# Moving TensorE's streamed operand as single elements taken in turn from its two halves

## The chip, the core and the metric

The kernel runs on one core of a Trainium2 chip. The metric is the device time of one execution in microseconds (us). The core has five engines that work side by side: TensorE (PE, matrix products), VectorE (DVE), ScalarE (ACT), GpSimd (POOL) and SyncE (SP, which issues most transfers). A matrix product on TensorE has two operands from SBUF: a block of 128x128 that is loaded into the array first (LDWEIGHTS, "PEld" in the profile), and a second one, up to 512 columns wide, that is moved through the array column by column (MATMUL, "PE"). The result lands in PSUM, from where VectorE or ScalarE read it.

## The reference

```python
def reference(q, k, v, w_in, w_out, s, b, w_gate, w1, w2):
    # masked attention: 4 batches, 8 heads, 576 positions, 64 dims
    scores = np.where(masks, q @ k.T / 8, -1e9)       # first 4 heads local, last 4 strided
    x = softmax(scores) @ v                           # -> [2304, 512]
    h = x @ w_in                                      # 512 -> 2048
    x2 = (s * np.maximum(h, 0) ** 2 + b) @ w_out      # 2048 -> 512
    logits = x2 @ w_gate                              # 8 experts, 288 tokens each, greedy by logit
    for e in range(8):
        out[mine(e)] = np.maximum(x2[mine(e)] @ w1[e], 0) @ w2[e]   # 512 -> 1024 -> 512
    return out
```

## The kernel before

Matrix products need more precision than one pass gives, so each float32 operand is split into a rounded high part and a low part (type float32r, 4 bytes per element), and three products (high x high, high x low, low x high) are summed in PSUM. All large products work in this way.

The order of the work is written out by hand, with generators that are advanced step by step (`Pipe`), so each engine's instructions stand in the order in which the code emits them. There are these stages:

- Attention (`attn_unit`, lines 222 to 312), in 32 units, beside the preparation of `w_in` and `w_out` (`prep`, lines 360 to 425). It uses many small matmuls.
- The first layer, `h_step` (lines 457 to 479): for each of 6 groups of 384 tokens and each of 16 blocks of 128 features, 12 matmuls at line 464 move a block of x (128x384). ScalarE reads PSUM with Relu (line 469), squares (line 470), and the result goes to a DRAM buffer `ud`.
- The second layer, `late_step` and `x2_late` (lines 638 to 684): `ud` comes back, is split (lines 653, 656), and line 683 issues the matmuls that `x2_list` (line 509) lists; they move a half-row block of `w_out` (128x512). Forty-eight of them are held for the end of this stage and are issued at line 895. `x2_row` (line 515) reads PSUM on VectorE (line 519). Beside this runs the choice of tokens for each expert (`route`, lines 729 to 863), whose small matmuls and VectorE steps are placed between those of line 683.
- Eight experts: `layer1` (line 935) issues 12 matmuls for each of 8 feature blocks (line 941, moving 128x288), `relu_split` (line 946) reads PSUM on ScalarE (line 947) and VectorE (line 948), and `expert` (line 950) issues 12 matmuls more for each block (line 966, moving 128x288), whose results are copied out at lines 974 and 976. The last expert (`last_expert`, line 996) has the second layer the other way round: line 1004 moves 128x512 of w2, and the results are copied out in two halves (lines 1009 and 1010).

All of these move their operand in the order in which it lies in SBUF. PSUM buffers are 8 tiles of 128x512, used in turn (`ps`, line 134).

Elsewhere the kernel has operands that are not read or written in the order in which they lie: `prep` reads the high or low word of pairs (lines 372, 378, 381: a step of 8 bytes), `attn_unit` writes the strided heads' results into `xb` with a step of 16 elements (line 310), and some reductions read across columns (lines 420 and 536 from PSUM, 757, 758 and 823 from SBUF).

Of the kernel before, what the change touches and what calls it, by code (L numbers as in the profile page):

```python
# [12 lines left out]
AF = mybir.ActivationFunctionType  # L13
ALU = mybir.AluOpType
# [14 lines left out]

def _f(ap):  # L30
    return ap.bitcast(F32)


class Pipe:
# [28 lines left out]
class Body:  # L63
# [262 lines left out]
    def group_x(self, g, dc):  # L326
        nc = self.nc
        S, G = self.S, self.G
        h = self.xs.tile([128, G], F32R, tag="xh", name=self.nm("xh"))
        l = self.xs.tile([128, G], F32R, tag="xl", name=self.nm("xl"))  # L330
        t = g * G
        while t < (g + 1) * G:
            b = t // S
            e = min((b + 1) * S, (g + 1) * G)
            src = self.xb[b][:, dc, t - b * S:e - b * S]
            o = slice(t - g * G, e - g * G)
            nc.scalar.copy(h[:, o], src)
            nc.vector.tensor_tensor(l[:, o], src, _f(h[:, o]), op=ALU.subtract)
            t = e
        self.xg.setdefault(g, {})[dc] = h, l  # L340
# [10 lines left out]
    def split(self, W, put):  # L351
        nc = self.nc
        h = self.wt([128, 512], F32R, "wh")
        l = self.wt([128, 512], F32R, "wl")
        nc.scalar.copy(h, W)  # L355
        yield
        nc.vector.tensor_tensor(l, W, _f(h), op=ALU.subtract)  # L357
        put((h, l))

    def prep(self, i):  # L360
# [10 lines left out]
        for r, h in zip(rv, half):  # L371
            nc.scalar.activation(_f(K[:, h]), _f(r[:, :, 1]), AF.Abs)
# [84 lines left out]
    def h_step(self, g, fc):  # L457
        nc = self.nc
        wh, wl = self.win[fc]
        ps = self.ps()  # L460
        k = 0
        for w, x in ((wh, 0), (wh, 1), (wl, 0)):
            for dc in range(4):
                nc.tensor.matmul(ps[:, :self.G], w[:, dc * 128:(dc + 1) * 128], self.xg[g][dc][x],  # L464
                                 start=(k == 0), stop=(k == 11))
                k += 1
        yield
        r = self.wt([128, self.G], F32, "r")
        nc.scalar.activation(r, ps[:, :self.G], AF.Relu)  # L469
        nc.scalar.activation(r, r, AF.Square)  # L470
        yield
        nc.sync.dma_start(self.ud[g][fc], r)
        if g in self.DG:
            return
        yield
        self.fold_step(fc, g, r)
        if fc == 15:
            yield
            yield from self.logits(g, self.pf[g])
# [28 lines left out]

    def x2_list(self, fc, acc, u, t=0):
        wh, wl = self.wout[fc]  # L510
        return [dict(out=acc[t + k], lhsT=u[:, j, k * 128:(k + 1) * 128], rhs=w,
                     start=(fc == 0 and i == 0), stop=(fc == 15 and i == 2))
                for k in range(u.shape[2] // 128) for i, (j, w) in enumerate(((0, wh), (0, wl), (1, wh)))]

    def x2_row(self, g, t, acc):
        nc = self.nc
        i = g * 3 + t
        row = self.Es[i % self.NE].rearrange("p c k -> p (c k)")
        nc.vector.scalar_tensor_tensor(row, acc[t], self.sb[:, 0:1], self.acc, op0=ALU.mult, op1=ALU.add)  # L519
        nc.sync.dma_start(self.x2d[i * 128:(i + 1) * 128, :], row)  # L520
        return row

# [412 lines left out]
    def layer1(self, fc, X, w1):  # L935
        ps = self.ps()
        fh, fs = fc // 4, (fc % 4) * 128
        k = 0
        for wi, xi in ((0, 0), (0, 1), (1, 0)):
            for dc in range(4):  # L940
                self.nc.tensor.matmul(ps[:, :288], w1[dc, fh][wi][:, fs:fs + 128], X[:, xi, dc, :],  # L941
                                      start=(k == 0), stop=(k == 11))
                k += 1
        return ps

    def relu_split(self, ps, h, l):
        self.nc.scalar.activation(h, ps[:, :288], AF.Relu)  # L947
        self.nc.vector.scalar_tensor_tensor(l, ps[:, :288], 0.0, _f(h), op0=ALU.max, op1=ALU.subtract)  # L948

    def expert(self, e, X, w1, w2):  # L950
        nc = self.nc
        y = []

        def step(fc):
            ps = self.layer1(fc, X, w1)
            yield
            u = self.p2.tile([128, 2, self.G], F32R, tag="u", name=self.nm("u2"), bufs=self.UB)
            self.relu_split(ps, u[:, 0, :288], u[:, 1, :288])
            yield
            if fc == 0:  # L960
                y.extend(self.ps() for _ in range(4))
            wh, wl = w2[fc]
            for dc in range(4):
                sl = slice(dc * 128, (dc + 1) * 128)
                for i, (w, j) in enumerate(((wh, 0), (wh, 1), (wl, 0))):
                    nc.tensor.matmul(y[dc][:, :288], w[:, sl], u[:, j, :288], start=(fc == 0 and i == 0),  # L966
                                     stop=(fc == 7 and i == 2))
            if fc < 7:
                return
            yT = []  # L970
            for dc in range(4):
                t = self.wt([128, 288], F32, "yT")
                if dc % 2:
                    nc.vector.tensor_copy(t, y[dc][:, :288])
                else:
                    nc.scalar.copy(t, y[dc][:, :288])
                yT.append(t)
            yield
            for c in range(3):
                ps = self.ps()  # L980
                for dc in range(4):
                    nc.tensor.transpose(ps[:96, dc * 128:(dc + 1) * 128], yT[dc][:, c * 96:(c + 1) * 96], self.identf)  # L982
                t = self.wt([96, 512], F32, "yr")
                if c % 2:
                    nc.vector.tensor_copy(t, ps[:96, :])
                else:
                    nc.scalar.copy(t, ps[:96, :])
                nc.gpsimd.indirect_dma_start(
                    out=self.a["out"][:, :],
                    out_offset=bass.IndirectOffsetOnAxis(ap=self.idx[:, 3 * e + c:3 * e + c + 1], axis=0),  # L990
                    in_=t, in_offset=None)
                yield

        return (step(fc) for fc in range(8))

    def last_expert(self, e, X, w1, w2):
        nc = self.nc
        us, y = [], []

        def layer2(fc, c):  # L1000
            if fc == 0:
                y.append(self.ps())
            for i, (j, w) in enumerate(((0, 0), (0, 1), (1, 0))):
                nc.tensor.matmul(y[c][:96, :], us[fc][j][:, c * 96:(c + 1) * 96], w2[fc][w],  # L1004
                                 start=(fc == 0 and i == 0), stop=(fc == 7 and i == 2))

        def put(c):
            t = self.Es[c].rearrange("p c k -> p (c k)")[:96]
            nc.scalar.copy(t[:, :256], y[c][:96, :256])
            nc.vector.tensor_copy(t[:, 256:], y[c][:96, 256:])  # L1010
            nc.gpsimd.indirect_dma_start(
                out=self.a["out"][:, :],
                out_offset=bass.IndirectOffsetOnAxis(ap=self.idx[:, 3 * e + c:3 * e + c + 1], axis=0),
                in_=t, in_offset=None)

        def step(fc):
            ps = self.layer1(fc, X, w1)
            yield
            u = [self.wt([128, 288], F32R, "u3") for _ in range(2)]
            self.relu_split(ps, u[0], u[1])  # L1020
            us.append(u)
            yield
            layer2(fc, 0)
            if fc == 7:
                put(0)
                for c in (1, 2):
                    for f in range(8):
                        layer2(f, c)
                    put(c)

        return (step(fc) for fc in range(8))
# [105 lines left out]
```

## Time and profile before

| | |
|---|---|
| median of 3 runs | 795.71 us (793.93 to 796.56) |
| the profiled execution | 795.12 us, of which span 793.3 us |
| TensorE busy | 771.1 us (97%), 6436 matmuls |
| weight loads busy | 677.9 us (85%) |
| VectorE busy | 493.4 us (62%) |
| ScalarE busy | 371.3 us (47%) |
| GpSimd busy | 52.4 us (7%) |
| mean granted TensorE clock | 0.992 |

The profile is one execution seen by the hardware profiler. The span runs from the first to the last instruction. Lines (L464) are lines of the kernel. Matmuls are pipelined, so a matmul's own duration holds its way through the array; the pace of a stream of them is read from their starts.

### The profile page before, as it was taken

What the parts mean: (1) busy time and instruction counts of PE and PEld (TensorE: products, weight loads), DVE (VectorE), ACT (ScalarE), POOL (GpSimd) and SP (SyncE); (2) the same over time, 40 slices, a digit from 0 to 9 for tenths busy, and PEclk for the clock granted to TensorE, in tenths of its full rate; (3) what the DMA queues carried; (4) which work ended last, traced back from release to release, by engine and by line L of the source; (5) the groups of instructions that cost most, each with busy time, mean ns of one, the idle gap of its engine ahead of it and who ended that gap; (6) DMA issues with size and microseconds to landing.
All of it is one profiled execution on the core that took longest, in us unless ns stands there. A gap on an engine that the chain in (4) does not pass through costs nothing.

```text
span 793.3 us, 16902 instructions
## 1 busy us (share of the span) xinstructions
PE 771.1 (97%) x6436; PEld 677.9 (85%) x6436; DVE 493.4 (62%) x1229; ACT 371.3 (47%) x893; POOL 52.4 (7%) x69
## 2 busy tenths in 40 slices
PE   7979999999999999999989999999999999999996
PEld 5769999999999878887767777778999999999994
DVE  8788997997650233267767778775456465555620
ACT  3787675666664554422222222230355454555520
POOL 1000000000000000000000000001102211321211
PEclk9989999999999999999999999999999999999999
DMA  6967846765774995535233523252857656755411
GB/s 175 266 212 239 265 139 201 239 207 189 250 260 170 318 300 195 165 120 175 91 132 122 177 89 100 81 160 68 239 169 222 208 162 213 214 176 170 130 31 30
DMA packets 88753, 140.19 MB, mean 177 GB/s; under 512 B 10849, under 2 KB 52577, under 8 KB 88673
## 3 DMA queue, kind: packets, MB, share of 16 engines
q1 hardware_dynamic: 85600, 129.68, 51.3%
q0 software_dynamic: 3072, 9.44, 3.7%
q8 instruction: 50, 0.82, 0.4%
q14 instruction: 31, 0.25, 0.1%
HBM read 106.32 MB, written 32.77 MB: 175 GB/s over the span
## 4 chain that ended last, share of the span: by engine, by line
PE 88%; DVE 4%; DMA 4%; ACT 1%; issue 1%; SPq 0%; POOLq 0%; DVEq 0%
PE b L464 25%; PE b L683 19%; PE b L941 13%; PE b L966 11%; PE b L242 3%; DMA r<-ud 3%; PE b L301 2%; PE b L502 2%; PE b L1004 1%; PE b L895 1%; PE b L982 1%; DVE E L519 1%; PE b L318 1%; PE b L397 1%; PE b L280 1%
## 5 line engine op out<-in xcount | busy, mean ns | idle before, releaser
L683 PE MATMUL b<-wh,u 128*128 128x512 f32 x544 | 176.9, 401 | 4.4 <-DVE u L656 4.4
L683 PEld LDWEIGHTS b<-wh,u 128*128 128x128 f32 x544 | 101.3, 190 | 25.4 <-DVE u L656 6.0
L653 ACT CAST u<-r 128x384 fp32r<-128x384 f32 (+1 forms) x96 | 47.5, 496 | 151.9 <-PE b L683 103.4
L683 PE MATMUL b<-wl,u 128*128 128x512 f32 x272 | 108.6, 399 | 0.0
L966 PE MATMUL b<-u,wh 128*128 128x288 f32 x448 | 93.5, 301 | 0.0
L464 PE MATMUL b<-xh,wh 128*128 128x384 f32 x384 | 87.4, 349 | 0.0
L469 ACT ACTIVATE r<-b 128x384 f32<-128x384 f32 x96 | 47.1, 490 | 83.7 <-PE b L464 80.0
L357 DVE TENSOR_TENSOR wl<-raw,wh 128x512 fp32r<-128x512 f32 x128 | 82.9, 684 | 0.3
L464 PE MATMUL b<-xl,wh 128*128 128x384 f32 x384 | 82.7, 336 | 0.0
L464 PE MATMUL b<-xh,wl 128*128 128x384 f32 x384 | 82.4, 335 | 0.0
L941 PE MATMUL b<-X,wh 128*128 128x288 f32 x512 | 78.4, 295 | 0.6 <-ACT X L914 0.6
L355 ACT CAST wh<-raw 128x512 fp32r<-128x512 f32 x128 | 73.6, 620 | 0.9 <-DVE u L656 0.5
L941 PEld LDWEIGHTS b<-X,wh 128*128 128x128 f32 x512 | 71.7, 188 | 1.4 <-ACT X L914 0.7
L464 PEld LDWEIGHTS b<-xh,wh 128*128 128x128 f32 x384 | 65.8, 189 | 6.8 <-issue 2.7
L966 PEld LDWEIGHTS b<-u,wh 128*128 128x128 f32 x448 | 70.9, 188 | 0.0
L948 DVE SCALAR_TENSOR_TENSOR u<-b,u 128x288 fp32r<-128x288 f32 x64 | 29.1, 455 | 66.7 <-ACT u L947 57.9
L464 PEld LDWEIGHTS b<-xl,wh 128*128 128x128 f32 x384 | 68.7, 189 | 0.0
L464 PEld LDWEIGHTS b<-xh,wl 128*128 128x128 f32 x384 | 68.3, 189 | 0.0
L966 PE MATMUL b<-u,wl 128*128 128x288 f32 x224 | 65.8, 294 | 0.0
L683 PEld LDWEIGHTS b<-wl,u 128*128 128x128 f32 x272 | 51.5, 190 | 9.4
L656 DVE TENSOR_TENSOR u<-r,u 128x384 fp32r<-128x384 f32 (+1 forms) x96 | 49.3, 530 | 15.7 <-ACT u L653 15.6
L947 ACT ACTIVATE u<-b 128x288 fp32r<-128x288 f32 x64 | 26.4, 412 | 58.9 <-PE b L941 55.1
(211 smaller groups left out, 1138.8 us busy)
## 6 DMA issues: line engine op xcount, KB each, us to landing
raw<-in_moe_w_dram SPq DMA_DIRECT2D x128, 256.0 KB
r<-ud SPq DMA_DIRECT2D x160, 192.0 KB
ud<-r SPq DMA_DIRECT2D x96, 192.0 KB
raw<-in_words_dram SPq DMA_DIRECT2D x64, 256.0 KB
qk<-in_q_dram SPq DMA_DIRECT2D x24, 288.0 KB
x2d<-E SPq DMA_DIRECT2D x18, 256.0 KB
wod<-K SPq DMA_DIRECT2D x16, 256.0 KB
wo<-wod SPq DMA_DIRECT2D x16, 256.0 KB
```

The lines of the kernel that those rows point to most:

```text
L242: nc.tensor.matmul(sp[64 * j:64 * j + p, c * kw:(c + 1) * kw], qk[sl, 0, q0:q0 + p], qk[sl, 1, k0:k0 + kw], start=after, stop=after or c = ...
L355: nc.scalar.copy(h, W)
L357: nc.vector.tensor_tensor(l, W, _f(h), op=ALU.subtract)
L464: nc.tensor.matmul(ps[:, :self.G], w[:, dc * 128:(dc + 1) * 128], self.xg[g][dc][x], start=(k == 0), stop=(k == 11))
L469: nc.scalar.activation(r, ps[:, :self.G], AF.Relu)
L653: nc.scalar.copy(d[:, 0, :], src)
L656: nc.vector.tensor_tensor(d[:, 1, :], src, _f(d[:, 0, :]), op=ALU.subtract)
L683: self.nc.tensor.matmul(**args)
L941: self.nc.tensor.matmul(ps[:, :288], w1[dc, fh][wi][:, fs:fs + 128], X[:, xi, dc, :], start=(k == 0), stop=(k == 11))
L947: self.nc.scalar.activation(h, ps[:, :288], AF.Relu)
L948: self.nc.vector.scalar_tensor_tensor(l, ps[:, :288], 0.0, _f(h), op0=ALU.max, op1=ALU.subtract)
L966: nc.tensor.matmul(y[dc][:, :288], w[:, sl], u[:, j, :288], start=(fc == 0 and i == 0), stop=(fc == 7 and i == 2))
```

## The change

Three helpers give views with two dimensions. `_alt(x)` reads columns 0, n/2, 1, n/2+1, 2, ...: one element of the first half, then one of the second. It is put around the moving operand of every large matmul (lines 464, 683 and 895 by way of `x2_list`, 941, 966, 1004). The blocks that are loaded as weights stay as they are. The results therefore stand in PSUM in that mixed order: column 2i holds element i, column 2i+1 holds element n/2+i. Every reader of them uses `_nat`, which reads the even columns and then the odd ones (a step of two floats), and writes to SBUF in natural order (`_two` only gives the other operands the same two dimensions). The counts of instructions, matmuls, transfers and waits are the same as before, and so is each one's size.

```diff
+def _alt(ap):
+    return ap.rearrange("p (t i) -> p i t", t=2)
+
+def _nat(ap):
+    return ap.rearrange("p (i t) -> p t i", t=2)
+
+def _two(ap):
+    return ap.rearrange("p (t i) -> p t i", t=2)
...
-                nc.tensor.matmul(ps[:, :self.G], w[:, dc * 128:(dc + 1) * 128], self.xg[g][dc][x],
+                nc.tensor.matmul(ps[:, :self.G], w[:, dc * 128:(dc + 1) * 128], _alt(self.xg[g][dc][x]),
...
-        nc.scalar.activation(r, ps[:, :self.G], AF.Relu)
+        nc.scalar.activation(_two(r), _nat(ps[:, :self.G]), AF.Relu)
...
-        return [dict(out=acc[t + k], lhsT=u[:, j, k * 128:(k + 1) * 128], rhs=w,
+        return [dict(out=acc[t + k], lhsT=u[:, j, k * 128:(k + 1) * 128], rhs=_alt(w),
...
-        nc.vector.scalar_tensor_tensor(row, acc[t], self.sb[:, 0:1], self.acc, op0=ALU.mult, op1=ALU.add)
+        nc.vector.scalar_tensor_tensor(_two(row), _nat(acc[t]), self.sb[:, 0:1], _two(self.acc), op0=ALU.mult, op1=ALU.add)
...
-                self.nc.tensor.matmul(ps[:, :288], w1[dc, fh][wi][:, fs:fs + 128], X[:, xi, dc, :],
+                self.nc.tensor.matmul(ps[:, :288], w1[dc, fh][wi][:, fs:fs + 128], _alt(X[:, xi, dc, :]),
...
-        self.nc.scalar.activation(h, ps[:, :288], AF.Relu)
-        self.nc.vector.scalar_tensor_tensor(l, ps[:, :288], 0.0, _f(h), op0=ALU.max, op1=ALU.subtract)
+        self.nc.scalar.activation(_two(h), _nat(ps[:, :288]), AF.Relu)
+        self.nc.vector.scalar_tensor_tensor(_two(l), _nat(ps[:, :288]), 0.0, _two(_f(h)), op0=ALU.max, op1=ALU.subtract)
...
-                    nc.tensor.matmul(y[dc][:, :288], w[:, sl], u[:, j, :288], start=(fc == 0 and i == 0),
+                    nc.tensor.matmul(y[dc][:, :288], w[:, sl], _alt(u[:, j, :288]), start=(fc == 0 and i == 0),
...
-                    nc.vector.tensor_copy(t, y[dc][:, :288])
+                    nc.vector.tensor_copy(_two(t), _nat(y[dc][:, :288]))
                 else:
-                    nc.scalar.copy(t, y[dc][:, :288])
+                    nc.scalar.copy(_two(t), _nat(y[dc][:, :288]))
...
-                nc.tensor.matmul(y[c][:96, :], us[fc][j][:, c * 96:(c + 1) * 96], w2[fc][w],
+                nc.tensor.matmul(y[c][:96, :], us[fc][j][:, c * 96:(c + 1) * 96], _alt(w2[fc][w]),
...
-            nc.scalar.copy(t[:, :256], y[c][:96, :256])
-            nc.vector.tensor_copy(t[:, 256:], y[c][:96, 256:])
+            v = _nat(y[c][:96, :])
+            nc.scalar.copy(t[:, :256], v[:, 0])
+            nc.vector.tensor_copy(t[:, 256:], v[:, 1])
```

## Rows read from the trace of the kernel before

**Rows 1.** The page's busy times: engine, us, share of the span, instructions.
```profile
PE 771.1 (97%) x6436; PEld 677.9 (85%) x6436; DVE 493.4 (62%) x1229; ACT 371.3 (47%) x893; POOL 52.4 (7%) x69
```

**Rows 2.** The page's chain that ended last, by engine and by line.
```profile
PE 88%; DVE 4%; DMA 4%; ACT 1%; issue 1%; SPq 0%; POOLq 0%; DVEq 0%
PE b L464 25%; PE b L683 19%; PE b L941 13%; PE b L966 11%; PE b L242 3%; DMA r<-ud 3%; PE b L301 2%; PE b L502 2%; PE b L1004 1%; PE b L895 1%; PE b L982 1%; DVE E L519 1%; PE b L318 1%; PE b L397 1%; PE b L280 1%
```

**Rows 3.** Stage windows: busy PE, PEld, DVE, ACT, POOL, then clock, DMA share, GB/s.
```profile
54.60:327.40 272.80, 272.55 (x2440) 246.83 (x2439) 168.53 (x433) 170.12 (x390) 1.88 (x9) 0.99 0.67 221
327.40:546.80 219.40, 214.14 (x1316) 164.77 (x1315) 159.40 (x433) 59.40 (x130) 0.00 (x0) 0.99 0.38 124
562.30:759.00 196.70, 196.70 (x1526) 196.52 (x1527) 113.01 (x211) 99.78 (x216) 38.55 (x39) 1.00 0.62 187
```

**Rows 4.** Groups by line, large matmuls: count, busy us, mean ns, idle before.
```profile
L683 PE MATMUL b<-wh,u 128*128 128x512 f32 x544 | 176.9, 401 | 4.4 <-DVE u L656 4.4
L966 PE MATMUL b<-u,wh 128*128 128x288 f32 x448 | 93.5, 301 | 0.0
L464 PE MATMUL b<-xh,wh 128*128 128x384 f32 x384 | 87.4, 349 | 0.0
L941 PE MATMUL b<-X,wh 128*128 128x288 f32 x512 | 78.4, 295 | 0.6 <-ACT X L914 0.6
L1004 PE MATMUL b<-wh,u 128*96 128x512 f32 x48 | 16.4, 399 | 0.0
L895 PE MATMUL b<-wh,ul 128*128 128x512 f32 x32 | 10.1, 392 | 0.0
```

**Rows 5.** Timelines of PE at full clock: start us, us, instruction, count.
```profile
61.81 0.85 PE L464 MATMUL b<-xl,wh 128*128 128x384 f32 x4
...
65.28 0.85 PE L464 MATMUL b<-xh,wh 128*128 128x384 f32 x4
...
416.42 0.62 PE L683 MATMUL b<-wh,u 128*128 128x512 f32 x2
...
417.10 0.62 PE L683 MATMUL b<-wh,u 128*128 128x512 f32 x2
```

**Rows 6.** Timeline of PE at 56 us, and one window there with its clock.
```profile
56.01 1.48 PE L464 MATMUL b<-xl,wh 128*128 128x384 f32 x4
57.29 1.08 PE L464 MATMUL b<-xh,wl 128*128 128x384 f32 x4
...
56.00:57.00 1.00, 1.00 (x5) 1.00 (x5) 1.00 (x4) 0.68 (x3) 0.00 (x0) 0.50 0.00 0
```

**Rows 7.** Groups by line, VectorE's reductions: count, busy us, mean ns.
```profile
L791 DVE TENSOR_REDUCE rt<-R 128x18 f32<-128x144 f32 x8 | 2.4, 302 | 0.0
L757 DVE TENSOR_REDUCE mm<-L 128x8 f32<-128x144 f32 x1 | 0.4, 418 | 0.0
L823 DVE TENSOR_REDUCE gsb<-rt 128x8 bf16<-128x144 bf16 x7 | 2.9, 411 | 0.2
L420 DVE TENSOR_REDUCE wog<-b 128x32 f32<-128x128 f32 x4 | 1.1, 287 | 19.7 <-PE b L418 19.7
```

**Rows 8.** Groups by line, ScalarE's copies and casts: count, busy us, mean ns.
```profile
L310 ACT COPY xb<-b 128x144 f32<-128x144 f32 x32 | 10.7, 444 | 0.3 <-PE b L301 0.3
L306 ACT COPY xb<-b 128x320 f32<-128x320 f32 x8 | 3.4, 427 | 0.0
L306 ACT COPY xb<-b 128x256 f32<-128x256 f32 x8 | 2.9, 368 | 0.0
L372 ACT ACTIVATE K<-raw 128x256 f32<-128x256 f32 x64 | 24.2, 427 | 0.0
L653 ACT CAST u<-r 128x256 fp32r<-128x256 f32 x16 | 6.5, 406 | 18.4 <-PE b L683 12.9 <-DMA r<-ud 3.8 <-DVE R L831 1.6
```

**Rows 9.** Groups by line, the most frequent reader of PSUM that changes.
```profile
L469 ACT ACTIVATE r<-b 128x384 f32<-128x384 f32 x96 | 47.1, 490 | 83.7 <-PE b L464 80.0 <-DMA r<-ud 2.1 <-PE b L502 1.5
```

## The prediction

> **What bounds the kernel now.** I read the busy times first: TensorE is busy for 97% of the span [rows 1]. A busy TensorE need not be the limit, so the chain of work that ended last comes next: 88% of it is TensorE, and the large matmuls of lines 464, 683, 941 and 966 alone are 68% [rows 2]. The third view, the stage windows, shows where another engine could hide anything: from 54.6 us on, TensorE has 0.25 us without work in the first layer, 5.3 us in the second and none in the experts, while VectorE and ScalarE are idle for a quarter to three quarters of each stage [rows 3]. So whatever one streamed column costs more or less goes into the time nearly in full, and what VectorE and ScalarE pay more is mostly covered.
>
> The fourth view is the pace of the stream, read from starts and not from durations (a matmul's own 300 to 400 ns hold its way through the array). At line 464 twenty matmuls of 384 columns, in five rows of four, start within 65.28 - 61.81 = 3.47 us: 173.5 ns each. At line 683 three of 512 columns (the row of one between the two shown is left out) start within 417.10 - 416.42 = 0.68 us: 226.7 ns [rows 5]. [...]
>
> **The change, part by part.** It adds no instruction, wait or transfer, and removes none; the queues keep their order. Two things change: how TensorE's moving operand is read, and how PSUM is read.
>
> *1. The moving operand.* How many columns are concerned: line 464 has three groups of 384 matmuls; each of the other lines has the group shown and one half as large with the low part of the weights: 544 + 272 at line 683, 32 + 16 at line 895, 512 + 256 at line 941, 448 + 224 at line 966, 48 + 24 at line 1004 [rows 4]. In columns: 1152 x 384 = 442,368; 864 x 512 = 442,368; 1440 x 288 = 414,720; 72 x 512 = 36,864; together 1,336,320 columns in 3528 matmuls. [...]
>
> The trace has no matmul whose moving operand jumps between elements, so its price is bounded by rows of other engines. VectorE reduces 144 elements in 302 ns where they lie side by side (line 791), and 144 elements in 418 ns where each is 32 bytes from the one before (line 757): 116 ns more, 0.81 ns per element. Bfloat16 elements 16 bytes apart give the same, 411 ns (line 823) [rows 7]. On ScalarE, line 306 writes 320 elements side by side in 427 ns and 256 in 368 ns, so 0.92 ns each, and 144 would take 265 ns; line 310 writes 144 with a step of 64 bytes and takes 444 ns: 1.24 ns more per element. But a step of 8 bytes is nearly free: line 372 reads 256 such elements in 427 ns, against 406 ns for 256 side by side (line 653) [rows 8]. So on two engines out of two, SBUF elements that are 16 bytes or more apart cost 0.8 to 1.2 ns more each, about 1.9 to 2.4 times the usual time of an element (VectorE's usual time from lines 791 and 420 [rows 7]: 302 - 287 = 15 ns for 16 elements, 0.94 ns each), and closer ones nothing much. After the change every element that TensorE moves is at least 576 bytes from the one before it (half of 288 columns of 4 bytes).
>
> From this the price on TensorE has three readings. (a) The lower bound: TensorE fetches ahead, and pays nothing: 0. (b) An access takes two of the engine's cycles instead of one, as VectorE and ScalarE show it in proportion: 0.416 ns more per column. (c) The upper bound: the price is a time of the memory and not of the engine: VectorE's element then takes about 0.94 + 0.81 = 1.75 ns, and TensorE's would too, 1.33 ns more per column. I take (b): it is the proportion of the rows, and lies between the ends. It gives 1,336,320 x 0.416 = 556 us more: 184 us each in the two layers, 173 us in the experts, 15 us in the last one's second layer.
>
> [...]
>
> [...] So the 13.4 ns x 3528 = 47 us may vanish in a slower stream or stay; I take half, -24 us, and keep 0 and -47 for the range.
>
> *2. The readers of PSUM.* Lines 469, 519, 947, 948, 974, 976, 1009 and 1010 now read PSUM with a step of 8 bytes. The nearest row is line 420, which reads 128 elements of PSUM 128 bytes apart in 287 ns, 15 ns less than the 144 side by side of line 791 [rows 7]: a step in PSUM costs VectorE nothing. The other bound is the SBUF price of 0.81 ns: line 469 would take 490 + 311 = 801 ns, 96 times, 30 us in all, in stages where ScalarE idles for about 100 us and where it waited 80 us for line 464 [rows 3, 9]. That is covered. Uncovered are only the last reader of the kernel, the one ahead of the first expert, and the edges between stages: at most 0.4 us each, 3 us in all. A gain is excluded, since no reader handles fewer elements. I take +2 us. [...]
>
> *3. What a slower stream hides.* TensorE's gaps between 54.6 and 759 us are some 6 us [rows 3]; where they wait for VectorE or a transfer, a slower stream covers them. I take -4 us.
>
> The sum: 793.3 + 556 - 24 + 2 - 4 = 1323 us of span, and with the 1.8 us that lie around the span, 1325 us. The profiled execution is 0.6 us below the median of the runs, so this needs no correction. For (b) alone the bounds are 795 + 556 - 47 - 6 = 1298 and 795 + 556 + 3 = 1354.
>
> **The rivals.** [...]
>
> *The price is a time of the memory* (c). VectorE's 1.75 ns and ScalarE's 0.92 + 1.24 = 2.16 ns are nearly equal in ns though their usual times differ, which speaks for it; the column would take about 1.75 ns: 795 + 1,336,320 x 1.33 ns = 2572 us.
>
> [...]
>
> *The change doesn't do what it says* would need a view that is folded back to the old order; the two halves can't be merged into one run, so I give it nothing of its own.
>
> **How the numbers follow.** (b) 0.42; TensorE doesn't pay 0.25; in between 0.15; time of the memory 0.17; anything else, a gain among it, 0.01. The forecast is (b), 1325 us. A difference of 0.3% (2.4 us) is what a measurement of this kernel can tell. The range reaches from the case without a price, 790, to the upper bound of (b), 1358: 0.82. The likeliest case's own range is 1298 to 1354. Of the free case, 0.22 is within 0.3% and 0.03 slower; so faster 0.01, same 0.22, slower 0.77.
>
> **What would show it.** Starts of 512-column matmuls at line 683 about 427 to 440 ns apart, of 384 columns 320 to 334 ns, with a granted clock that stays at 1.0: (b). 227 and 173.5 ns: free. About 900 ns: (c). Line 469 near 490 ns shows that stepped PSUM reads are free; near 800 ns that they aren't. VectorE's and ScalarE's busy times should stay within some us, and their waits for TensorE should grow. The forecast is wrong if the pace in order is kept, or if the clock drops to 0.50 as well, which would make the small matmuls slower too.

## The result, and the profile after

The changed kernel takes 762.69 us (median of 4 runs, 761.94 to 762.89) against 795.16 us: a ratio of 0.9596, 95% interval 0.9578 to 0.9614. It is 32 us faster, where 1325 us were forecast and 790 was the lower end of the range. The profiled execution has a span of 760.1 us.

The first view is the pace of the stream, as in [rows 5]. Timelines of PE in the changed kernel (start us, us, instruction, count; line 476 is line 464 of before, line 695 is 683):

```profile
62.35 0.81 PE L476 MATMUL b<-xl,wh 128*128 128x384 f32 x4
...
64.95 0.81 PE L476 MATMUL b<-xh,wl 128*128 128x384 f32 x4
...
419.29 0.60 PE L695 MATMUL b<-wh,u 128*128 128x512 f32 x2
...
421.23 0.59 PE L695 MATMUL b<-wh,u 128*128 128x512 f32 x2
```

Sixteen matmuls of 384 columns (four rows of four) start within 64.95 - 62.35 = 2.60 us, 162.5 ns each, against 173.5 [rows 5]. Nine of 512 columns start within 421.23 - 419.29 = 1.94 us, 215.6 ns each, against 226.7. A column still takes 0.415 ns (53.1 ns for 128 columns, against 53.2 before); what is gone is about 11 ns per matmul at both widths.

The stage windows (columns as in [rows 3]: busy time and count of PE, PEld, DVE, ACT and POOL, then clock, DMA share, GB/s), cut where the stages now end:

```profile
55.00:319.10 264.10, 263.35 (x2441) 235.70 (x2439) 172.89 (x434) 174.25 (x390) 1.93 (x9) 0.99 0.69 228
319.10:529.10 210.00, 202.94 (x1316) 164.74 (x1315) 159.65 (x433) 59.13 (x130) 0.00 (x0) 1.00 0.40 130
544.10:727.60 183.50, 183.50 (x1527) 183.45 (x1528) 113.13 (x211) 99.51 (x216) 37.88 (x39) 1.00 0.66 201
```

Against [rows 3] the first layer is 8.7 us shorter, the second 9.4 us, the experts 13.2 us. The readers of PSUM cost what they cost before (groups by line, line 481 is 469):

```profile
L481 ACT ACTIVATE r<-b 128x384 f32<-128x384 f32 x96 | 46.9, 489 | 68.2 <-PE b L476 66.4 <-PE b L514 0.6
```

489 ns against 490 [rows 9], and ScalarE waits less for TensorE: 66 us in place of 80.

### The profile page after: what moved, and what is told of

The parts are those of the page before. It is cut to its first block, busy times and chain, and to the rows that moved or that the text cites. A ratio compares the mean times of both kernels' runs of the same rounds, so it can differ in the third digit from the quotient of the medians.

```text
span 760.1 us, 16927 instructions
## 1 busy us (share of the span) xinstructions
PE 735.5 (97%) x6436; PEld 653.4 (86%) x6436; DVE 498.1 (66%) x1229; ACT 374.8 (49%) x893; POOL 51.6 (7%) x69
## 4 chain that ended last, share of the span: by engine, by line
PE 83%; DVE 9%; DMA 3%; issue 2%; ACT 2%; SPq 0%; POOLq 0%; DVEq 0%
PE b L476 22%; PE b L695 19%; PE b L953 12%; PE b L978 11%; PE b L254 3%; PE b L514 2%; DMA r<-ud 2%; PE b L313 2%; PE b L1016 1%; PE b L907 1%; DVE E L531 1%; PE b L994 1%; PE b L330 1%; PE b L941 1%; PE b L292 1%
## 5 line engine op out<-in xcount | busy, mean ns | idle before, releaser
L695 PE MATMUL b<-wh,u 128*128 128x512 f32 x544 | 169.5, 387 | 5.5 <-DVE u L668 5.5
L695 PE MATMUL b<-wl,u 128*128 128x512 f32 x272 | 105.1, 387 | 0.0
L978 PE MATMUL b<-u,wh 128*128 128x288 f32 x448 | 87.9, 294 | 0.0
L476 PE MATMUL b<-xh,wh 128*128 128x384 f32 x384 | 83.2, 340 | 0.0
L476 PE MATMUL b<-xh,wl 128*128 128x384 f32 x384 | 78.8, 328 | 0.3 <-DVE wl L369 0.3
L476 PE MATMUL b<-xl,wh 128*128 128x384 f32 x384 | 78.8, 329 | 0.0
L953 PE MATMUL b<-X,wh 128*128 128x288 f32 x512 | 73.4, 287 | 0.6 <-ACT X L926 0.6
L953 PEld LDWEIGHTS b<-X,wh 128*128 128x128 f32 x512 | 67.4, 189 | 1.3 <-ACT X L926 0.7
L476 PEld LDWEIGHTS b<-xl,wh 128*128 128x128 f32 x384 | 65.6, 191 | 0.0
L482 ACT ACTIVATE r<-r 128x384 f32<-128x384 f32 x96 | 50.5, 526 | 3.0
```

The source lines that it names most:

```text
L695: self.nc.tensor.matmul(**args)
L978: nc.tensor.matmul(y[dc][:, :288], w[:, sl], _alt(u[:, j, :288]), start=(fc == 0 and i == 0), stop=(fc == 7 and i == 2))
```

## The experiments

**1. One chain per pattern.** So that the price of a pattern stands by itself, the first kernel runs chains of 48 matmuls, each with new weights, with nothing beside them.

```diff
+            return v.rearrange("p (t i r) -> p i t r", t=2, r=r)
...
+        def alt512(ps, k, st, sp):
+            mm(ps, w(k), alt(x(k)), start=st, stop=sp)
+        self.chain(N, alt512)
...
+            mm(ps, w(k), x(k).rearrange("p (i t) -> p t i", t=2), start=st, stop=sp)
...
```

> This kernel leaves the whole computation out: it writes zeros and runs 29 chains of 48 matmuls, one way of reading or writing per chain, with nothing else on the chip beside them. Read is the pace, start to start, of each chain. Seen so far: 512 columns in order took 226.7 ns each, and in the changed kernel about 216 ns, so some 11 ns per matmul are gone. Theory A (every jump to another 16-byte line counts: single elements from two halves, whatever the rest): chains with single elements from 2, 4 or 64 places 216 ns; even columns and then odd ones, and runs of 4 or more elements in turn, 227 ns. Theory B (any pattern with two dimensions does it, one plain run doesn't): every chain with two dimensions 216 ns, also runs of 128 and two rows of 256; only plain runs 227 ns. Theory C (the weight load and the plain read of 4-byte elements get in each other's way): the cost of plain reads goes down with narrower weights (64, 32 columns: 221 and 218 ns) and is absent with bfloat16, where both orders take about 216 ns. Theory D (the 11 ns were due to the other engines and transfers of the full kernel): all chains alike here, 216 ns. By all of them the part is the same ns at 288, 384 and 512 columns.

The chain of work of this kernel is simply the sequence of its pieces (start us, us, instruction, count). For 512 columns: line 1196 in order, 1088 halves in turn, 1108 even columns and then odd ones, 1112 runs of 2 from the halves, 1116 runs of 4, 1128 runs of 128, 1132 two separate rows of 256, 1136 four quarters in turn, 1140 sixty-four places in turn, 1148 in order with weights of 32 columns, 1160 and 1164 in order from 1 and 4 elements further on, 1172 and 1176 in order and halves in turn with weights that are read with a step of 16 bytes, 1188 bfloat16 with its halves in turn. Lines 1092 and 1096 are 384 columns in order and in turn, 1100 and 1104 the same for 288. The first chain, line 1084, is in order too (46 matmuls in 12.06 us); it holds the start of the work on TensorE and is not used.

```profile
36.02 10.36 PE b L1088 x48
46.38 8.34 PE b L1092 x48
54.71 7.80 PE b L1096 x48
62.51 6.33 PE b L1100 x48
68.84 5.88 PE b L1104 x48
74.72 21.66 PE b L1108 x48
96.38 16.01 PE b L1112 x48
112.38 12.00 PE b L1116 x48
...
147.43 10.92 PE b L1128 x48
158.34 10.88 PE b L1132 x48
169.22 13.57 PE b L1136 x48
182.79 20.69 PE b L1140 x48
...
214.51 11.12 PE b L1148 x48
...
247.42 11.36 PE b L1160 x48
258.77 11.12 PE b L1164 x48
...
290.50 11.27 PE b L1172 x48
301.78 11.35 PE b L1176 x48
...
333.86 23.25 PE b L1188 x48
...
367.48 10.91 PE b L1196 x48
```

Divided by 48: in order 227.3 ns, halves in turn 215.8; for 384 columns 173.8 and 162.5, for 288 columns 131.9 and 122.5. So the gain is there without any other engine, and theory D falls. It is 11.5 ns at 512 columns, 11.3 at 384 and 9.4 at 288, where all four theories had the same ns. Two dimensions alone do nothing (two rows 226.7, runs of 128 227.5): B falls. Narrower weights don't help (231.7 with 32 columns): C falls in that part. And a jump on every column isn't the point either, A falls: four quarters in turn take 282.7, sixty-four places 431.0, even and then odd columns 451.2, about twice the usual time. Bfloat16 with its halves in turn is the slowest of all, 484.4.

The even-then-odd chain is the one that shows the price which the prediction had expected: there every column is 8 bytes from the last, and yet a matmul takes twice as long (451.2 ns against 227.3), while with jumps of 1024 bytes there and back it takes less (215.8). That leads to theory E, a supposition that the next kernel tests: TensorE fetches the odd and the even columns as two separate streams. By it, in the even-then-odd chain, each stream steps by 16 bytes; with the halves in turn, each stream reads its half in order.

The weights are not without influence: with weights read in steps of 16 bytes, the halves in turn take 236.5 ns and the operand in order 234.8, so the gain is gone. And in order from 4 elements further on takes 231.7 ns, though the number of 16-byte pieces is the same. E explains neither.

**2. The two streams.** The second kernel of chains chooses the two places freely.

```diff
+            mm(ps, w(k), pat(k, (1, 256), (4, 2)), start=st, stop=sp)
...
+            mm(ps, w(k), pat(k, (2, 256), (640, 2)), start=st, stop=sp)
...
+            mm(ps[:, :256], w(k), pat(k, (4, 256)), start=st, stop=sp)
```

> Leaves the whole computation out, writes zeros, and runs chains of 48 matmuls (16 for plain float32), one pattern per chain. The first chains gave, for 512 float32r columns: in order 227 ns, halves in turn 216, even then odd columns 451, runs of 2 from the halves 333, of 4 250, four quarters in turn 283. Theory E (odd and even columns are fetched by two separate streams, each of which needs about 1.67 ns per new 16 bytes; in order each stream needs 128 fetches, 213 ns, as long as the columns take, so a start-up of 11 ns is never caught up; with halves in turn 64 fetches leave slack): distances between the two places of 4 to 1024 elements all near 216; every element twice 216; two places 640 apart, each with a step of 2, 227 (128 fetches per stream); 256 columns with a step of 4, 225 to 240 (128 fetches for 107 ns of columns); 256 columns in order 118 to 120, in turn 109. Theory G (the two places must lie far apart in the memory): distances 4 to 64 near 227 or worse; step 2 at two far places 216. Theory H (any pattern whose inner dimension is two far elements helps): step 2 at two places 216, small distances 227. Bfloat16 (in order 215, halves in turn 484): by E, with pairs of 2-byte elements as the unit, runs of 2 from the halves 215, even-then-odd 450 or more. Plain float32: no difference beyond 11 ns by any theory.

The pieces of its chain (as above). Line 1089: places 4 elements apart, 1125: 1024 apart, 1129: 257 apart, 1133: every element twice, 1137: two places with a step of 2, 1141: 256 columns with a step of 4, 1149 and 1153: 256 columns in order and in turn, 1157 and 1161 the same for 128. Line 1165 is plain float32 in order, 1169 its halves in turn; 1174 to 1186 are bfloat16: in order, runs of 2, runs of 4, even then odd.

```profile
42.13 10.36 PE b L1089 x48
...
135.37 10.36 PE b L1125 x48
145.73 10.36 PE b L1129 x48
156.09 10.36 PE b L1133 x48
166.45 10.90 PE b L1137 x48
177.35 11.20 PE b L1141 x48
...
198.94 5.76 PE b L1149 x48
204.70 5.36 PE b L1153 x48
210.06 5.31 PE b L1157 x48
215.37 5.35 PE b L1161 x48
220.73 13.79 PE b L1165 x32
234.52 17.28 PE b L1169 x32
251.79 10.36 PE b L1174 x48
262.15 13.01 PE b L1178 x48
...
286.04 10.84 PE b L1186 x48
```

All eleven distances, from 4 to 1024 elements and odd 257 among them, take 10.36 us, 215.8 ns: where the two places lie doesn't matter, and G and H fall. Two far places with a step of 2 take 227.1 ns, the pace in order, as E says. 256 columns with a step of 4 take 233.3 ns, about twice their 106.7 ns of columns (0.4167 ns each, from lines 1088 and 1104 of the first kernel: 10.36 - 5.88 = 4.48 us for 48 times 224 columns). The price of a fetch can be estimated, by theory E, from line 1108 of the first kernel and 1141: (451.2 - 233.3) / (256 - 128) = 1.70 ns for each new 16 bytes of a stream. By this estimate a stream in order needs 128 of them for 512 columns, 218 ns, a little more than the 213 ns of the columns; with the halves in turn 64, 109 ns, less than the columns, and what remains is 2.5 ns beyond them. The fetches alone do not make up the 227.3 ns: 9 ns are left in order, and 15 in lines 1108 and 1141. E calls them a start-up, which slack in the fetches hides; that is argued and not shown.

The gain shrinks with the length. For 256 columns it is 8.3 ns (120.0 and 111.7, where E had 109 for the second), and for 128 there is none (110.6 and 111.5).

Bfloat16 in order (line 1174) and float32r with the halves in turn are both at 215.8 ns; float32r in order, 227.3, is not. Counted by theory E, a fetch that brings one element gives about half the pace (line 1108, 451.2 ns), and with two elements per fetch, float32r in order, a matmul is still 11 ns late.

What E didn't get right: for bfloat16 I had taken pairs as the unit, with 215 ns for runs of 2 and 450 or more for even-then-odd; measured are 271.0 and 225.8 ns. With single elements as the unit the 225.8 fits (8 bytes per step, two elements per fetch), but then the halves in turn should be fast, and they take 484.4. Nor does E give the size of the runs of 2 and 4 of float32r (333.5 and 250.0 ns) or of the four quarters in turn (282.7 ns), where by it each stream jumps between two places. Why these cost what they do stays open, so E is the theory that fits the most chains, and not one that is shown in full. Plain float32 loses by the change: 540 ns in place of 431 per recorded matmul.

**3. One line of the kernel alone.**

```diff
...
-                nc.tensor.matmul(ps[:, :self.G], w[:, dc * 128:(dc + 1) * 128], self.xg[g][dc][x],
+                nc.tensor.matmul(ps[:, :self.G], w[:, dc * 128:(dc + 1) * 128], _alt(self.xg[g][dc][x]),
...
-        nc.scalar.activation(r, ps[:, :self.G], AF.Relu)
+        nc.scalar.activation(_two(r), _nat(ps[:, :self.G]), AF.Relu)
```

> Only line 464 (1152 matmuls of 384 columns) and its reader are changed; everything else reads in order. If the pace of the chains carries over (173.8 to 162.5 ns for 384 columns), 1152 x 11.3 ns = 13 us less at most; the first layer of the changed kernel was 8.7 us shorter, so 783 to 788 us against 795. If the gain came from PSUM readers, or from the stages helping each other, no such sum: within 2 us of 795, or below 780.

783.54 us against 794.5, ratio 0.9856 (0.9825 to 0.9887): 11 us less, where the chains allow 13 at most. In its trace the first layer is 262.6 us long and thus 10.2 us shorter than in [rows 3]:

```profile
54.60:317.20 262.60, 261.70 (x2440) 235.39 (x2439) 172.68 (x433) 174.28 (x390) 1.93 (x9) 0.99 0.69 229
```

The other lines were not changed alone.

**4. Four quarters in the whole kernel.**

```diff
 def _alt(ap):
-    return ap.rearrange("p (t i) -> p i t", t=2)
+    return ap.rearrange("p (t i) -> p i t", t=4)
```

(with `_nat`, `_two` and the last copies to match.)

> The changed kernel, but with single elements in turn from four quarters and not from two halves. If every single-element jump were as good as the change (theory A), 763 us. By the pace of the chains (282.7 ns against 227 for 512 columns, 0.109 ns per column more, 1,336,320 columns) 795 + 145 = 940 us, a little less where TensorE waits today.

901.29 us. The sign and the order of size are as the chains say, so it isn't single elements as such that help. The forecast of 940 took the chain's price at 512 columns for all: in the kernel twenty-eight matmuls of 512 columns of line 695 take 7.70 us, 275 ns each, and 384 columns take 205 ns (four rows of four start within 68.72 - 65.44 = 3.28 us), 31 ns more than in order and not 42. The lines are of its timeline of PE and of its chain of work.

```profile
65.44 0.98 PE L476 MATMUL b<-xh,wl 128*128 128x384 f32 x4
...
68.72 0.98 PE L476 MATMUL b<-xh,wh 128*128 128x384 f32 x4
...
543.56 7.70 PE b L695 x28
```

**5. The readers alone, and another pattern with the same number of fetches by theory E.**

```diff
 def _alt(ap):
-    return ap.rearrange("p (t i) -> p i t", t=2)
+    return ap
```

> Only the readers of PSUM are changed (a step of two floats), and TensorE moves its operand in order, so the results stay in a mixed order and the output isn't the reference's. By theory E the whole gain is in the moved operand and the stepped reads cost nothing: 795 us, within 2 us, and the Relu reader of line 469 stays at 490 ns. If the readers had a part in the gain or took some of it away: 5 us or more on either side.

794.79 us against 793.75, ratio 1.0011 (0.9996 to 1.0026), and its Relu reader takes 491 ns:

```profile
L481 ACT ACTIVATE r<-b 128x384 f32<-128x384 f32 x96 | 47.1, 491 | 83.3 <-PE b L476 82.3 <-PE b L514 1.0
```

Reading PSUM with a step of two floats costs nothing that can be told here (2 us at most by the interval), and it has no part in the gain.

```diff
 def _alt(ap):
-    return ap.rearrange("p (t i) -> p i t", t=2)
+    return ap.rearrange("p (b t i) -> p b i t", t=2, i=4)
...
 def _nat(ap):
-    return ap.rearrange("p (i t) -> p t i", t=2)
+    return ap.rearrange("p (t i) -> p t i", t=2)
```

> All large matmuls move single elements in turn from two places 4 elements apart, in blocks of 8 (0, 4, 1, 5, 2, 6, 3, 7, 8, 12, ...); the readers of PSUM read in order, so the results stay in a mixed order and the output isn't the reference's. By theory E each of the two streams still needs one fetch per four of its elements, as with the halves: 760 to 765 us, with 216 ns per 512 columns. If it has to be two far halves: 795 us. If a change of pattern every 8 columns costs something, as with runs of 8 from the halves (243 ns against 227): above 800.

761.22 us against 793.75, ratio 0.9591 (0.9575 to 0.9607): the same as the change, with the same pace (its timeline of PE):

```profile
63.13 0.81 PE L476 MATMUL b<-xl,wh 128*128 128x384 f32 x4
...
65.73 0.49 PE L476 MATMUL b<-xh,wl 128*128 128x384 f32 x2
```

Sixteen matmuls (four rows of four) start within 2.60 us, 162.5 ns each. No far halves are needed; by E, only that each stream finds its elements side by side, four for each 16 bytes. Here the kernel does what E forecast.

**6. What is missing in the first layer.**

```diff
-            nc.vector.tensor_tensor(self.acc, self.acc, W, op=ALU.add)
+            nc.gpsimd.tensor_tensor(self.acc, self.acc, W, op=ALU.add)
```

> The changed kernel, with one VectorE step of the preparation (the 15 additions to acc, 10.3 us in the first layer) given to GpSimd, to see whether the missing 4 us of the first layer (13 us expected from its 1152 matmuls, 8.7 us seen) hang on VectorE. If they do: 757 to 761 us. If they hang on transfers or on the matmuls between: 762 to 764. If GpSimd's slower additions hold up the end of the preparation: above 765.

761.93 us, ratio 0.9601 (0.9585 to 0.9617): no difference from the change. So these 10.3 us of VectorE's work are not what holds the first layer. By the chains' paces the change is worth 1152 x 11.3 + 864 x 11.5 + 1440 x 9.4 + 72 x 11.5 ns = 13.0 + 9.9 + 13.5 + 0.8 = 37 us, and 33 us came in the span; some 4 of the rest are in the first layer. The waits of the weight loads there show one part of it (who waited for whom: us in all, times, longest), before and after:

```profile
PEld b L502 <- DMA r<-ud: 1.9, 4, 0.9
```

```profile
PEld b L514 <- DMA r<-ud: 4.5, 9, 0.9
```

The matmuls of line 502 (514 after) wait 2.6 us longer for the loads of `ud`. The other part was not found, and some of it may be no more than the difference between two executions: with places 4 elements apart the first layer is 262.2 us long, 10.6 us less than before, in a kernel with the same time as the change.

```profile
55.50:317.70 262.20, 261.95 (x2440) 236.04 (x2439) 168.02 (x433) 169.45 (x389) 1.93 (x9) 0.99 0.70 229
```

## Why the prediction was wrong

*In short.* The term that failed is the price of the moving operand, +556 us. No column became dearer (0.416 ns before, 0.415 after), and about 11 ns per matmul went, which made the kernel 32 us faster.

*What bounds the kernel* was right: TensorE's stream, so that a change of its pace goes into the time nearly in full. 33 of the 37 us did.

*The price per column.* The 0.416 ns come from [rows 5]: 226.7 - 173.5 = 53.2 ns for 128 columns. The +556 us count them a second time for each column, as a second cycle of the engine. No run shows the cycles that reading (b) counts, nor a second 0.416 ns; the runs show 0.416 ns per column before and 0.415 after, at a granted clock of 0.99 to 1.00.

*The fixed part.* The -24 us are half of 13.4 ns for each of 3528 matmuls: what 512 columns of 0.4167 ns leave of 226.7 ns, taken as a part that the order of the operand doesn't touch. No run shows such a part of 13.4 ns; the runs show that 11 of it go with the order (226.7 to 215.6 ns in the kernel), and in the chain with the halves in turn 2.5 are left. Taking it as fixed was the mistake, and two rows could have raised the doubt. In [rows 6], at a granted clock of 0.50, four matmuls of 384 columns start within 57.29 - 56.01 = 1.28 us, 320 ns each: 0.833 ns per column, twice the 0.4167 of full clock, with nothing left over. I read this as a part that may vanish in a slower stream, but it also fits a limit beside TensorE's own clock that is about as fast as the columns at full clock (0.416 ns each). That row alone doesn't decide it. And the kernel's bfloat16 matmuls, which the prediction leaves out (timeline of PE before):

```profile
10.70 1.15 PE L318 MATMUL b<-mstr,identb 128*128 128x288 bf16 x8
11.69 0.29 PE L235 MATMUL b<-mstr,identb 128*128 128x288 bf16 x1
```

Eight of 288 columns start within 0.99 us, 123.8 ns each: the pace that float32r reaches only after the change (122.5), and not the 131.9 it has in order. A fixed part that one type pays and the other doesn't is no fixed part.

*The price of the step.* Rows 7 and 8 were read rightly as such: 144 elements took VectorE 411 ns at 16 bytes from one to the next and 418 at 32, against 302 side by side, and ScalarE 444 at 64 bytes; by the prediction's estimates 1.75 ns each on VectorE and about 2.2 on ScalarE. The estimate for a stream of TensorE, 1.70 ns, is close to VectorE's; that both have one cause, a time of the memory as in reading (c), is not shown by any run. As by theory E two streams share the columns, a column would then take half of it, and even columns and then odd ones bring in the chain the doubling that was forecast (451.2 ns). What failed was the word "before" in "from the one before it": by theory E the distance that counts is not that to the column before, but that to the column two before, in the same stream, and by that measure the change reads in order. For two places in turn it is shown that the distance to the column before does not count: 4 to 1024 elements all take 215.8 ns.

*The bounds.* The lower bound of the operand's price was put at 0 with no reason that excluded a gain, though the trace had no such operand at all, and the chance of a gain was 0.01. The upper bound of (b) is 1354 us in the sum and 1358 in the range, a slip that changes nothing. Reading (a), by which nothing is paid and the time stays at 795 us, came nearest, though it too has no gain in it.

*The readers* were right: 489 ns, and alone a ratio of 1.0011, within the noise. *The fixed part going with a slower stream* (-24 us) and *the gaps that it covers* had no object. *The clock* stayed at full speed: 0.99 to 1.00 in the stages.

## What to carry to other kernels

A term that looks fixed per instruction should be compared across types and clock levels in the same trace before it is called fixed; here two rows would have put the 13 ns in doubt. In these runs float32r matmuls gained 9 to 11 ns each (227.3 to 215.8, 5%, at 512 columns; 131.9 to 122.5, 7%, at 288), but nothing at 128 columns (110.6 and 111.5), where the odd columns were read side by side and the even ones too; the readers of PSUM undid the order at no cost that showed (794.79 us against 793.75). Do not carry it to weights that are read with a step (236.5 in place of 234.8 ns), nor to bfloat16 or plain float32, where the same pattern costs 484 in place of 216 and 540 in place of 431 ns, and where no row shows what a pattern costs, leave both signs open.

## What the runs showed of the hardware that was not expected

- Even columns and then odd ones, a step of only 8 bytes, halve the pace of float32r (451.2 ns for 512 columns against 227.3 in order), while a step of 8 bytes costs ScalarE little (427 ns against 406 for 256 elements [rows 8]).
- Three steps of the preparation that read raw words with a step of 8 bytes became slower when line 464 took its halves in turn (384 of after is 372 of before, 390 is 378, 393 is 381), though nothing of them was changed:

```profile
L384 ACT ACTIVATE K<-raw 128x256 f32<-128x256 f32 x64 | 28.5, 497 | 0.0
L390 DVE SCALAR_TENSOR_TENSOR W<-raw,K 128x256 int32<-128x256 int32 x64 | 26.4, 454 | 1.3
L393 DVE SCALAR_TENSOR_TENSOR K<-raw,W 128x256 int32<-128x256 int32 x64 | 26.3, 451 | 0.0
```

  The first takes 497 ns against 427 [rows 8], the others 454 against 422 and 451 against 418. For the first it is 493 ns with line 464 alone changed, 428 with only the readers of PSUM changed, 426 with places 4 elements apart and 431 with four quarters, so it hangs on the moved operand. The kernel with places 4 elements apart has the gain without this loss and the same time, so the loss costs nothing here; why it happens is open.
